# The first loads of a transformer-block kernel: block 3 of x on ScalarE's queue, V's first weights one transfer sooner

## The chip, the cores and the metric

The kernel runs on one core of a Trainium2 chip. Its time is the device time of one execution in microseconds (us), as the median of several runs. A profile of one execution comes with it: its span is counted from the first instruction of the program to the last, and a little time lies around it. Engines are named as in the profile: PE (matmul), PEld (its weight loads), DVE (vector), ACT (scalar, activation functions), POOL (GpSimd) and SP (issues most of the DMAs). "SPq" and "ACTq" are the queues in which SP and ACT issue DMAs.

## The reference

The kernel computes, for one sequence of 2048 rows of 640 values in bfloat16, the row-normalized input xn, and then the sum of x, an attention branch and a gated feed-forward branch, both fed by xn. The attention has 32 heads of 20 values and a sliding window of 256 positions.

```
def _layernorm(x, axis=-1, eps=1e-5):
    m = jnp.mean(x, axis=axis, keepdims=True)
    v = jnp.var(x, axis=axis, keepdims=True)
    return (x - m) / jnp.sqrt(v + eps)
...
        qkv = (x @ wqkv)                   # split in q, k, v of 32 heads
        p = _softmax(where(window of 256, q k^T * 20**-0.5))
        return (p v) @ wo
...
        h = _sigmoid(x @ w_gate) * (x @ w_up)      # 640 -> 1536
        return h @ w_down
...
    xn = _layernorm(A_x)
    return A_x + _A_ref(xn, A_wqkv, A_wo) + _B_ref(xn, ...)
```

## The kernel before

The 2048 rows are worked through in four chunks of 512 rows, and a chunk is four blocks of 128 rows. The order of instructions on every engine is that of the program text (a manual schedule); the framework adds the waits. Only the start of the program matters here, the first chunk until its V projection is done; after that a list of steps interleaves the attention of one chunk with projections and feed-forward work of others, so that PE has always something to do.

**Loads.** The first chunk of x is loaded block by block: `load_rows(s, queue)` (line 156) moves block s, 128 rows of 640 values (160 KB), on the queue that it is given. `load_v(hf)` (line 160) moves one half of V's weights, 400 KB, on SP. `load_wqkv(0)` and `(1)` (line 151) move q's and k's weights, 800 KB each, and then the gate and up weights follow (line 180) and two stores of zeros into scratch (line 177, `clear`). All of these are issued by SP, in this order: block 0, block 1, block 3, V's first half, block 2, V's second half, q, k, gate, up.

**POOL** fills zeros (line 173: 128 partitions of 1536 values, the source of `clear`), makes the identity matrix that the transposes need, fills `neghalf` and `eps` (lines 217 and 219), and then the constant parts of four V tiles (lines 347 and 348).

**ACT** loads the table of the square root and runs a dummy square root on `eps` (line 221), so that the table is there before it is needed.

**PE** first runs eleven dummy matmuls on a constant (line 226, `keep_busy`).

**Normalization of the first chunk** (lines 673 to 710). Blocks 0 and 3 take their statistics on DVE (line 252, two halves of 320 values each, and line 258), the root on ACT (`root`, line 649), the reciprocal and the normalization on DVE (lines 653 and 271). Blocks 1 and 2 take the mean and the sum of squares on ACT (`mean_act`, line 659; `root_act`, lines 664 and 665) and reciprocal and normalization on DVE (lines 669 and 670). Each block is then transposed by five PE instructions (line 277) and copied out of PSUM (line 278: block 0 by ACT in two pieces, the others by DVE). V of a block needs its transposed rows and V's weights: `project_v` (line 353), five matmuls for each half of the weights; the result is copied by ACT or DVE (line 364).

The order of the text interleaves these, and each engine's own order follows from it. DVE: statistics of block 0, normalization of block 0, first half of block 3's statistics, normalization of block 1, second half of block 3's statistics, copy of block 1's transposes, normalization of block 3, and so on. ACT: mean of block 1, root of block 0, squares and root of block 1, copies of block 0's transposes, root of block 3, mean, squares and root of block 2, then copies. PE: dummy matmuls, transposes of block 0, two dummy matmuls, transposes of block 1, V of block 0 (first half of the weights, called v00 below), V of block 1 (first half), transposes of block 3, V of block 0 (second half, v01), V of block 1 (second half), then block 3 with the transposes of block 2 in between, then block 2, and then the q and k projections (line 324).

Each DMA tells of its landing through a semaphore that counts to 16, one for each of 16 DMA engines.

Of the kernel before, what the change touches and what calls it, by code (L numbers as in the profile page):

```python
# [9 lines left out]
P = 128  # L10
# [17 lines left out]
EPS = 1e-5  # L28
# [10 lines left out]
FP32 = mybir.dt.float32  # L39
# [54 lines left out]
def kernel(  # L94
# [11 lines left out]
    nc = tc.nc  # L106
# [4 lines left out]
    def pool(name, bufs, **kw):  # L111
        return ctx.enter_context(tc.tile_pool(name=name, bufs=bufs, **kw))

    const = pool("const", 1)
# [40 lines left out]
    def load_rows(s, queue):  # L155
        queue.dma_start(out=xc[0][:, s, :], in_=xr[:, s, :])  # L156

    def load_v(hf):
        a = hf * HALF
        nc.sync.dma_start(out=wqkv[2][:, :, a:a + HALF], in_=wqkv_r[:, :, 2 * D + a:2 * D + a + HALF])  # L160

    load_rows(0, nc.sync)
    load_rows(1, nc.sync)
    load_rows(3, nc.sync)
    load_v(0)
    load_rows(2, nc.sync)
    load_v(1)
# [1 line left out]
    load_wqkv(1)  # L169

    scratch = {w: tc.dram_tile([H * 32, CW], BF16, name="s" + w) for w in "qk"}
    zero = kp.tile([P, GH, CW], BF16, name="kT")
    nc.gpsimd.memset(zero[:, 0:3, :], 0.0)

# [40 lines left out]
    make_identity(nc, ident)  # L215
    neghalf = const.tile([P, SBC], FP32, name="neghalf")
    nc.gpsimd.memset(neghalf, -0.5)
    eps = const.tile([P, 1], FP32, name="eps")
    nc.gpsimd.memset(eps, EPS)
    scr = const.tile([P, 1], FP32, name="scr")  # L220
    nc.scalar.activation(out=scr, in_=eps, func=SQRT)

    def keep_busy(widths):
        ps = ps_d.tile([P, CW], FP32, name="pwarm", tag="d")
        for n in widths:
            nc.tensor.matmul(ps[:, 0:n], lhsT=ones[:, 0:P], rhs=ones[:, 0:n], start=True, stop=True)
# [623 lines left out]
```

## Time and profile before

| what | value |
| --- | --- |
| median of 3 runs | 308.06 us (308.03 to 308.24) |
| the profiled execution's own time | 308.12 us |
| its span | 306.4 us |
| PE busy | 299.8 us, 98% of the span |
| ACT, DVE, POOL busy | 199.2, 177.6, 177.0 us |
| DMA | 36.87 MB, 120 GB/s on average |
| granted TensorE clock | full throughout |

How to read it: busy times are sums over the whole span. The timeline gives start and duration of an instruction in us from the span's start, its engine, line, operation, the tile that it writes, an arrow and the tiles that it reads, and in brackets the engine's idle time ahead of it with what ended it. The chain of waits is followed back from the last instruction to end: each line has a start, a duration and what the time was spent on. A stretch of the table of windows gives the busy time of each engine in it, the granted clock, the mean busy share of the 16 DMA engines, and the GB/s that they moved.

### The profile page before, as it was taken

Reading aid. Unit: us, or ns where it says so; the run is one execution under the profiler, and the core shown is the slowest. Engines: PE = TensorE matmul, PEld = TensorE weight load, DVE = VectorE, ACT = ScalarE, POOL = GpSimd, SP = SyncE. Lnnn points to the kernel's source line nnn. Section 1 sums busy time; section 2 is a strip of 40 time slices with the busy share of each in tenths; the row PEclk is TensorE's granted clock in tenths of the full one; section 3 lists DMA queues with packets and bytes.
Section 4 is the critical chain, followed back from the end, with each engine's and each line's share of the span. In section 5 each row is a group of like instructions: output and inputs, shape, how many; then the busy total and the mean of one; then the engine's idle time right before and its main releaser. Section 6 shows DMA issues by size and latency. Waiting matters only on the chain.

```text
span 306.4 us, 10016 instructions
## 1 busy us (share of the span) xinstructions
PE 299.8 (98%) x4290; PEld 165.4 (54%) x4325; DVE 177.6 (58%) x355; ACT 199.2 (65%) x198; POOL 177.0 (58%) x317
## 2 busy tenths in 40 slices
PE   7999999999999999999999999999999999999996
PEld 3654444445657654554557654554546665444775
DVE  5735539879675564496946464483733626372434
ACT  6933877698854649888674647878585547778000
POOL 3174687687982927676682728557382847657000
PEclk9999999999999999999999999999999999999999
DMA  7997977886427052810046212740000210000202
GB/s 204 364 328 259 300 201 220 313 242 203 156 90 171 21 181 68 263 50 2 2 132 131 66 58 71 249 142 0 2 2 2 68 43 25 2 2 2 88 21 68
DMA packets 40174, 36.87 MB, mean 120 GB/s; under 512 B 8864, under 2 KB 39840, under 8 KB 40096
## 3 DMA queue, kind: packets, MB, share of 16 engines
q1 hardware_dynamic: 39264, 35.46, 37.6%
q10 hardware_dynamic: 864, 0.75, 0.8%
q8 instruction: 34, 0.56, 0.7%
q14 instruction: 12, 0.10, 0.1%
HBM read 25.59 MB, written 11.44 MB: 121 GB/s over the span
## 4 chain that ended last, share of the span: by engine, by line
PE 96%; DMA 2%; issue 1%; SPq 0%; ACT 0%; ACTq 0%; DVE 0%
PE y L472 18%; PE pu L456 17%; PE pg L449 17%; PE pqk L324 14%; PE ps L529 9%; PE pv L353 7%; PE y L480 7%; PE acc L562 6%; DMA wv<-in_A_wqkv_dram 2%; SPq L156 0%; ACT th L821 0%; PE pt L277 0%; ACTq L496 0%; DVE xn L484 0%
## 5 line engine op out<-in xcount | busy, mean ns | idle before, releaser
L546 POOL TENSOR_SCALAR_AFFINE_SELECT pT<-pT 64x512 bf16<-64x512 bf16 (+1 forms) x256 | 157.0, 613 | 83.4 <-ACT pT L535 71.0
L535 ACT ACTIVATE pT<-ps 128x2048 bf16<-128x2048 f32 (+1 forms) x76 | 141.0, 1855 | 59.4 <-PE ps L529 58.7
L460 DVE SCALAR_TENSOR_TENSOR h<-th,pu 128x512 bf16<-128x512 f32 x48 | 32.7, 680 | 49.8 <-PE pu L456 44.2
L456 PE MATMUL pu<-xnT,wu 128*128 128x512 bf16 x228 | 59.0, 380 | 0.7 <-issue 0.2
L449 PE MATMUL pg<-xnT,wg 128*128 128x512 bf16 x226 | 58.5, 380 | 1.0 <-issue 0.3
L472 PE MATMUL y<-wd,h 128*128 128x320 bf16 (+3 forms) x407 | 56.6, 292 | 0.0
L472 PEld LDWEIGHTS <-h 128*128 128x128 bf16 x407 | 37.1, 98 | 15.3 <-issue 1.8
L452 ACT ACTIVATE th<-pg 128x512 f32<-128x512 f32 x48 | 28.6, 595 | 15.5 <-PE pg L449 15.4
L449 PEld LDWEIGHTS <-wg 128*128 128x128 bf16 x240 | 22.2, 98 | 25.8 <-issue 1.8
L456 PEld LDWEIGHTS <-wu 128*128 128x128 bf16 x240 | 22.0, 98 | 25.5 <-issue 2.0
L529 PE MATMUL ps<-qT,kT 20*64 20x320 bf16 (+4 forms) x1440 | 32.1, 260 | 0.0
L574 DVE STREAM_TRANSPOSE t<-acc 128x512 f32<-128x512 f32 x32 | 21.1, 697 | 17.3 <-PE acc L562 17.3
L529 PEld LDWEIGHTS <-kT 20*64 20x64 bf16 x1440 | 15.4, 103 | 25.0 <-issue 22.4
L484 DVE SCALAR_TENSOR_TENSOR rows<-y,rows 128x320 bf16<-128x320 f32 x30 | 14.5, 487 | 22.9 <-PE y L480 22.7
L586 DVE TENSOR_TENSOR on<-t,rec 128x320 bf16<-128x320 f32 (+4 forms) x48 | 26.0, 542 | 1.1
L353 PE MATMUL pv<-wv,xnT 128*128 128x320 bf16 x160 | 25.6, 300 | 0.1
L480 PE MATMUL y<-wo,oc 128*128 128x320 bf16 (+2 forms) x165 | 24.2, 295 | 0.0
L324 PE MATMUL pqk<-xnT,wk 128*128 128x512 bf16 x97 | 23.0, 380 | 0.2
L324 PE MATMUL pqk<-xnT,wq 128*128 128x512 bf16 x94 | 22.7, 380 | 0.4 <-issue 0.2
L364 DVE CAST v<-pv 64x320 bf16<-64x320 f32 x29 | 14.1, 485 | 11.7 <-PE pv L353 11.4
L562 PE MATMUL acc<-pT,v 64*32 64x320 bf16 (+4 forms) x1440 | 19.7, 253 | 0.0
L562 PEld LDWEIGHTS <-v 64*32 64x32 bf16 x1440 | 16.2, 91 | 5.8 <-issue 1.6
(54 smaller groups left out, 195.4 us busy)
## 6 DMA issues: line engine op xcount, KB each, us to landing
qT<-sq SPq DMA_DIRECT2D x16, 256.0 KB
kT<-sk SPq DMA_DIRECT2D x16, 256.0 KB
sq<-st SPq DMA_DIRECT2D x20, 128.0 KB
sk<-st SPq DMA_DIRECT2D x20, 128.0 KB
out_dram<-rows SPq DMA_DIRECT2D x15, 160.0 KB
wg<-in_B_w_gate_dram SPq DMA_DIRECT2D x4, 480.0 KB
wu<-in_B_w_up_dram SPq DMA_DIRECT2D x4, 480.0 KB
xc<-in_A_x_dram SPq DMA_DIRECT2D x3, 640.0 KB
```

What stands on the lines that cost most here:

```text
L324: nc.tensor.matmul(ps, lhsT=wt[:, m, :], rhs=xnT[c][:, d, :], start=(d == 0), stop=(d == DC - 1))
L353: nc.tensor.matmul(ps[:, 0:HALF], lhsT=xnT[c][:, d, s * P:(s + 1) * P], rhs=wqkv[2][:, d, hf * HALF:(hf + 1) * HALF], start=(d == 0), stop ...
L449: nc.tensor.matmul(pg, lhsT=part(wg, d, f), rhs=xnT[c][:, d, :], start=(d == 0), stop=(d == DC - 1))
L452: nc.scalar.activation(out=th, in_=pg, func=TANH, scale=0.5)
L456: nc.tensor.matmul(pu, lhsT=part(wu, d, f), rhs=xnT[c][:, d, :], start=(d == 0), stop=(d == DC - 1))
L460: nc.vector.scalar_tensor_tensor(out=h, in0=th, scalar=1.0, in1=pu, op0=ADD, op1=MULT)
L472: nc.tensor.matmul(y[:, lo:lo + width], lhsT=ht[c, f][:, s * P:(s + 1) * P], rhs=wd[:, f, cut[0] + lo:cut[0] + lo + width], start=(f == 0) ...
L480: nc.tensor.matmul(y[:, 0:cut[1] - cut[0]], lhsT=oc[c, m][:, s * P:(s + 1) * P], rhs=wo[:, m, cut[0]:cut[1]], start=False, stop=(m == DC - 1))
L529: nc.tensor.matmul(ps[a * U:(a + 1) * U, i, col * U:(col + n) * U], lhsT=qk["k", kc, o // GH][32 * i:32 * i + DH, o % GH + a, kb * U:(kb + ...
L535: nc.scalar.activation(out=pt[:, :, 0:width], in_=ps[:, :, 0:width], func=EXP, scale=SCALE)
L546: nc.gpsimd.affine_select(out=view, in_=view, pattern=[[0, HG], [0, n], [sign, U]], compare_op=GE, fill=0.0, base=base, channel_multiplier ...
L562: nc.tensor.matmul(acc[32 * i:32 * i + 32, q * U:(q + n) * U], lhsT=vt[kb][a * U:(a + 1) * U, u, h * VW:h * VW + 32], rhs=pt[a * U:(a + 1) ...
```

## The change

Three edits, all in the first loads.

- Block 3 of the first chunk is no longer the third load on SP. It is issued by ACT's queue, in the text right behind the dummy square root. On SP, V's first half is now the third load, and everything behind it moves up by one.
- `eps` is filled by POOL ahead of the zeros instead of behind `neghalf`.
- The same instructions run on PE and DVE in the same order. ACT has one more instruction, the DMA issue, between the dummy square root and the mean of block 1; it carries no wait. Lines below the edit shift by up to one in the changed file.

```
     load_rows(0, nc.sync)
     load_rows(1, nc.sync)
-    load_rows(3, nc.sync)
     load_v(0)
     load_rows(2, nc.sync)
     load_v(1)
...
     scratch = {w: tc.dram_tile([H * 32, CW], BF16, name="s" + w) for w in "qk"}
+    eps = const.tile([P, 1], FP32, name="eps")
+    nc.gpsimd.memset(eps, EPS)
     zero = kp.tile([P, GH, CW], BF16, name="kT")
     nc.gpsimd.memset(zero[:, 0:3, :], 0.0)
...
     nc.gpsimd.memset(neghalf, -0.5)
-    eps = const.tile([P, 1], FP32, name="eps")
-    nc.gpsimd.memset(eps, EPS)
     scr = const.tile([P, 1], FP32, name="scr")
     nc.scalar.activation(out=scr, in_=eps, func=SQRT)
+    load_rows(3, nc.scalar)
```

More of the change, by code (lines that the diff above doesn't have):

```diff
@@ L163 @@
     load_rows(1, nc.sync)
-    load_rows(3, nc.sync)
     load_v(0)
@@ L171 @@
     scratch = {w: tc.dram_tile([H * 32, CW], BF16, name="s" + w) for w in "qk"}
+    eps = const.tile([P, 1], FP32, name="eps")
+    nc.gpsimd.memset(eps, EPS)
     zero = kp.tile([P, GH, CW], BF16, name="kT")
@@ L217 @@
     nc.gpsimd.memset(neghalf, -0.5)
-    eps = const.tile([P, 1], FP32, name="eps")
-    nc.gpsimd.memset(eps, EPS)
     scr = const.tile([P, 1], FP32, name="scr")
     nc.scalar.activation(out=scr, in_=eps, func=SQRT)
+    load_rows(3, nc.scalar)
     def keep_busy(widths):
```

## Prediction

> **What bounds the kernel now.** I read the page first: PE is busy for 299.8 of 306.4 us, and the chain that ended last is PE for 96% and DMA for 2%. So time can be won or lost only where PE stands still. I listed its gaps: all are ahead of 7.1 us, except some of 0.05 or 0.16 us, where a matmul record is missing ("x4" for five), and the drain of the last stores. The rest is a full queue: a shift of PE at 11 us arrives whole at the end, unless a new wait swallows it. So I worked out only the first 11 us.
>
> The chain in order of time, for the first 12 us:
>
> ```profile
> 1.71 0.43 SPq L156
> 2.14 0.04 issue
> 2.18 4.88 DMA wv<-in_A_wqkv_dram
> 7.06 0.04 issue
> 7.10 1.52 PE pv L353 x10
> 8.62 0.28 PE pt L277 x5
> 8.90 1.77 PE pv L353 x13
> 10.66 0.28 PE pt L277 x5
> ```
>
> The first V matmul (v00) starts when the first half of V's weights lands, 7.06. That load is SP's fourth issue, behind three 160 KB blocks of x; the block-3 issue ahead of it is the 1.71 line. Removing it brings V's issue from 2.18 to 1.71: 0.47 us. But see how little is behind the wait, in the timeline:
>
> ```profile
> 5.25 0.49 DVE L252 BATCH_NORM_STATS2 stats<-xc 128x6 f32<-128x320 bf16 x1
> ...
> 5.50 0.29 ACT L665 ACTIVATE rstd<-rstd,eps 128x1 f32<-128x1 f32 x1
> ...
> 5.83 0.16 DVE L669 RECIPROCAL rstd<-rstd 128x1 f32<-128x1 f32 x1
> ...
> 6.03 0.45 DVE L670 TENSOR_SCALAR xn<-xc,neg,rstd 128x640 bf16<-128x640 bf16 x1
> ...
> 6.53 0.45 PE L277 MATMUL pt<-ident,xn 128*128 128x128 bf16 x5 [0.41 <-DVE xn L670]
> ...
> 7.10 1.52 PE L353 MATMUL pv<-wv,xnT 128*128 128x320 bf16 x10
> ```
>
> The five transposes of block 1, ahead of v00 in PE's queue, start at 6.53. Such a run occupies PE 0.28 us before a V matmul follows (the chain's 8.62 0.28). So v00 could start at 6.81: the weights hold it for **0.29 us, and no more can be won there**, though the load comes 0.47 sooner. Behind the weights stands block 1: landed by 3.64 (ACT's wait ends there), then ACT's mean, square and root, DVE's normalization, the transposes, each instruction released by the one before. A block 1 late by d makes v00 possible at 6.81+d.
>
> **Next waits on PE's way.** The ten V matmuls and block 3's transposes keep their own pace: transposes 1.36 us after v00, the next V matmuls (v01, second half of the weights) 0.28 later. By the trace's semaphore counts that second half landed complete at 8.61, and v01 started at 8.74, so without a sooner landing only 0.09 can be passed on there (8.61+0.04=8.65). Block 2's transposes stand 1.76 after v01, at 10.50; their input was written at 9.85+0.45=10.30, and 0.06 later (as from 6.03+0.45 to 6.53, rounded up) is 10.36. That chain goes back through ACT (root 7.15, mean of block 2 at 7.51) to DVE's statistics of block 3. It moves with d, except for 0.07: ACT was free at 7.44 and block 2 landed at 7.49. So block 2's transposes cannot start before 10.29+d: 0.21 us before today with d=0. **The end moves by the larger of PE's own shift and d-0.21.**
>
> **Part by part.**
> 1. Epsilon ahead of the zeros. POOL does the same instructions; the 0.10 us memset goes from 2.67 to about 0.80. The zeros, 1.38 us, identity and V memsets come up to 0.10 later at first. The identity is ready at 2.69 and used at 5.39; the zeros' DMA is issued at 8.73. No cost, cover over 2 us. The gain is on ACT: its dummy SQRT waits for epsilon 0.72 us, to 2.80; ACT's next input comes at 3.64, so of itself this saves nothing. It frees the DMA issue written behind the SQRT.
> 2. One ACT issue more: 0.36 to 0.45 us (the four at 282.98 to 284.81). Block 1 is not there before 3.64, so an issue ending by then costs ACT nothing; held to 2.8 it would still end at 3.25.
> 3. SP: one issue fewer. V's first weights 0.47 sooner, block 2, V's second half, wq, wk likewise up to the 1.66 us issue at 4.27, where the queue is full (the DMAs are busy 0.98 and more from 5 us on). Each still has its landing bound by the bytes ahead.
> 4. When does block 3 start? Unshown: no ACT issue stands behind a table load in this trace. The nearest row is this:
>
> ```profile
> 281.75 1.88 ACT L535 ACTIVATE pT<-ps 128x2048 bf16<-128x2048 f32 x1 [0.87 <-PE ps L529]
> 282.98 0.87 ACTq L491 DMA_DIRECT2D rows<-in_A_x_dram  x2
> 283.52 0.59 ACT L452 ACTIVATE th<-pg 128x512 f32<-128x512 f32 x1
> ```
>
> The tanh at 283.52 is ahead of the DMAs in ACT's program. Its wait for PE ended at 282.87; then ACT's queue issued the DMA at 282.98, while the exp still ran and the tanh had not begun. So a wait holds the queue, a busy engine does not. Early bound: epsilon done at 0.90, block 3 issued at about 1.0, beside the table load (0.80 to 2.09). Late bound: the load holds it, 2.1 to 2.3. I take the **early one**, nearest to that row. Then block 3 is no longer behind block 1 (SP issue 1.25) but ahead of it.
>
> 5. What that does to block 1. Busy share of the DMAs and GB/s are the last two columns here:
>
> ```profile
> 1.75:2.00 0.25, 0.25 (x2) 0.05 (x1) 0.00 (x0) 0.25 (x1) 0.25 (x1) 1.00 0.41 61
> 2.00:2.25 0.25, 0.25 (x2) 0.15 (x1) 0.00 (x0) 0.09 (x1) 0.25 (x2) 1.00 0.66 143
> 2.25:2.50 0.25, 0.25 (x2) 0.00 (x0) 0.00 (x0) 0.00 (x0) 0.17 (x2) 1.00 1.03 369
> ...
> 2.75:3.00 0.25, 0.25 (x2) 0.07 (x1) 0.00 (x0) 0.20 (x1) 0.25 (x7) 1.00 1.00 369
> ...
> 3.75:4.00 0.25, 0.25 (x2) 0.15 (x1) 0.23 (x1) 0.25 (x1) 0.00 (x0) 1.00 0.47 54
> 4.00:4.25 0.25, 0.25 (x2) 0.04 (x1) 0.21 (x1) 0.25 (x1) 0.00 (x0) 1.00 0.55 105
> ```
>
> From 2.25 to 3.5 the engines are nearly full. Before 2.25 some 51 thousand bytes moved ((61+143)x0.25); the other 440 of the three blocks' 491 take 1.19 us at 369 GB/s: the last byte at 3.44. In this trace the last packet of the three ended at 3.77 and block 3 landed at 4.08, 0.31 behind; block 1, issued last of the three, would land at 3.44+0.31=3.75 against 3.62: **d=0.13**, between 0 (block 3 takes only idle time) and 0.46 (block 1 lands where block 3 did, 4.08; issue to landing was 2.37 us for both). Block 0 may be late by 0.15 at no cost: its statistics end at 4.23, and its root waits for ACT until 4.38.
> Beside it, a sentence that carries nothing: the Trainium skill, "DMA: Bandwidth & Descriptors", section "Issuing engines are not separate DMA queues", says that transfers from either issuer interleave on the same 16 engines and only issue time is saved; it speaks against the gain, and by it alone the weights would land with the same bytes ahead of them and the sum would come to no change.
>
> **Sum** with d=0.13: V's first weights, 0.47 sooner less some sharing, land between 6.59 and 7.06; if by 6.90, v00 starts at 6.81+0.13=6.94. Block 3's transposes follow at 8.30, v01 at 8.58 (8.65 if the second half still lands at 8.61), so PE could reach block 2's transposes at 10.34 to 10.41; their input lets them start at 10.29+0.13=10.42 against 10.50: **-0.08 us**. The profiled execution is 308.12 (span 306.41 and 1.71 around it), 0.06 over the median of 308.06; so 308.04 for it, 308.0 for the median.
>
> **Rivals.**
> - A, the forecast: most of the gain is lost to the later block 1; over d=0.1 to 0.46 the end moves by -0.1 to +0.25: 307.95 to 308.3, from d=0.21 on no gain. Chance 0.55.
> - B, the gain comes: block 3 uses idle engines (the 0.47 and 0.55 shares at 3.75 to 4.25 speak for it) or is issued at 2.1 and lands 2.37 later, 4.5, before its use at 5.25. Then d=0, v00 at 6.81, and the end moves by -0.09 (second half still at 8.61) to -0.21: 307.85 to 307.97. Against it: full engines. Chance 0.25.
> - C, slower: block 3 is issued at 2.1 or later, and the engines serve V's first weights ahead of it. DVE needs block 3 at 5.25 and has 0.09 to spare (5.74 to 5.83) before block 1's reciprocal, which is queued behind; then block 1's transposes and v00 wait. Block 3 landing at r gives d=r-5.34; it decides from r=5.55, costs 0.2% from 6.17, and at worst (V's 6.59 plus 0.44 for its own eight packets per engine, 55 ns each in the trace) r=7.03, +1.48: 309.5. For it: block 2, behind V's weights on SP, took 4.83 us. Against it: a separate queue, and the early issue. Chance 0.13, half of it beyond 0.2%.
> The Trainium skill, same page, section "Queues, rings and completion order", has an engine drain a run of some 9 to 17 descriptors of one ring before it switches; that rule leans to C. No run here shows two rings sharing yet.
> - D, it does nothing: V's weights land at 7.06 as now, since the bytes ahead are the same, and d is under 0.2; 308.06. Chance 0.07.
>
> About 0.2% (0.6 us) is what a measurement of this kernel can tell from no change. A, B and D lie inside; beyond it are half of C and some unforeseen delay of the first loads. PE's gaps before 7.1 us make a gain of 0.6 all but impossible. Slower 0.10, faster 0.02, same 0.88. Range: A and B, and C up to its half, 307.8 to 308.6.
>
> **What would show it.** In the changed profile: ACT's DMA issue beside the table load (1.0) or behind it (2.1); the start of ACT's mean of block 1 (3.64 now: d directly); V's issue at 1.71; the first V matmul (6.94 in A, 6.81 in B, over 7.1 in C); block 2's transposes against 10.50, and the same difference at the end. DVE's statistics of block 3 later than 5.25 with block 1 on time would mean C. A different shift at the end than at 10.50 would refute that the rest is a full queue.

## The result, and the profile after

| | before | after |
| --- | --- | --- |
| median of the runs | 307.96 us (307.89 to 308.24) | 309.05 us (308.92 to 310.14) |
| the profiled execution's own time | 308.12 us | 308.92 us |
| its span | 306.4 us | 307.2 us |
| granted TensorE clock | full throughout | full throughout |

The changed kernel is slower: the ratio of the times is 1.0038, with an interval from 1.0026 to 1.005. The medians differ by 1.09 us, the two profiled executions by 0.80. That of before lay 0.16 above its median and that of after 0.13 below, so the two traces account for 0.80, and the other 0.29 is spread over executions that left no trace.

The chain of waits of after, for its first 12 us (start, duration, what the time was spent on), no longer begins with V's weights:

```profile
1.25 3.12 DMA xc<-in_A_x_dram
4.37 0.02 issue
4.39 0.83 ACT xn L659 x2
5.22 0.19 ACT rstd L649
5.41 0.82 ACT xn L664 x2
...
6.78 0.46 DVE xn L670
7.24 0.05 issue
7.29 0.45 PE pt L277 x5
7.74 1.44 PE pv L353 x10
9.18 0.28 PE pt L277 x5
9.46 1.77 PE pv L353 x13
11.22 0.28 PE pt L277 x5
```

Before, the end hung on a load that SP issued at 2.18 and that landed at 7.06. Now it hangs on block 1, issued at 1.25 and landed at 4.37, and on everything that is done to it: mean, root, squares, normalization, transposes. V's weights do not appear any more. The timeline shows the same from the side of the instructions:

```profile
0.80 1.28 ACT L220 ACT_TABLE_LOAD   x1 [0.80 <-PEq L834]
0.94 0.38 ACTq L156 DMA_DIRECT2D xc<-in_A_x_dram  x1
...
3.54 0.89 DVE L252 BATCH_NORM_STATS2 stats<-xc 128x6 f32<-128x320 bf16 x2 [3.54 <-DMA xc<-in_A_x_dram]
4.39 0.74 ACT L659 ACTIVATE xn<-xc 128x640 bf16<-128x640 bf16 x1 [2.10 <-DMA xc<-in_A_x_dram]
```

ACT's queue issued block 3 at 0.94, while the table load ran (0.80 to 2.08). The mean of block 1 began at 4.39 and not at 3.64: block 1 was late by 0.75. Block 0's statistics began at 3.54, where they began at 3.10 before: block 0 was late too. From the semaphore counts of the two traces, the times at which the last of 16 counts came:

| landed complete | before | after |
| --- | --- | --- |
| block 0 | 3.08 | 3.52 |
| block 3 | 4.08 | 3.93 |
| block 1 | 3.62 | 4.37 |
| V's weights, first half | 7.06 | 6.27 |
| block 2 | 7.49 | 6.72 |
| V's weights, second half | 8.61 | 7.85 |

So the change did what its text says: V's first half came 0.79 sooner. But block 3 was served whole between block 0 and block 1. From block 0 to block 1 it took 0.54 before and 0.85 after, 0.31 more; the other 0.44 of the 0.75 is that block 0 itself came later. The table of windows shows that part. Its last two columns are the busy share of the DMAs and the GB/s, as in the prediction's table of before:

```profile
1.75:2.00 0.25, 0.25 (x2) 0.05 (x1) 0.00 (x0) 0.25 (x1) 0.25 (x1) 1.00 1.02 92
2.00:2.25 0.25, 0.25 (x2) 0.15 (x1) 0.00 (x0) 0.24 (x2) 0.25 (x2) 1.00 0.66 97
2.25:2.50 0.25, 0.25 (x3) 0.00 (x0) 0.00 (x0) 0.05 (x1) 0.17 (x2) 1.00 0.54 97
2.50:2.75 0.25, 0.25 (x2) 0.15 (x1) 0.00 (x0) 0.00 (x0) 0.25 (x3) 1.00 0.63 179
2.75:3.00 0.25, 0.25 (x2) 0.07 (x1) 0.00 (x0) 0.00 (x0) 0.25 (x7) 1.00 1.03 379
```

Where before reached 369 GB/s at 2.25, after moved 97, and 179 in the quarter behind it, although there was more to move. The packets show how: of those that began before 2.6 us, 12 took over 300 ns, up to 764, where before had one, of 331; the usual packet of a block takes 55. Three other kernels with one queue (the runs with one more instruction on ACT, with `eps` alone and with the order 0, 3, 1) had 4 to 7 such packets, none over 382: the change brings longer ones more than it brings more of them.

With that, block 2's transposes began at 11.06 instead of 10.50. From there on PE's shift stayed at 0.55 up to 46 us. Then a **second part** came: from 48.96 to the end the shift is 0.80. It begins at the exp on ACT that frees PSUM for PE's scores. ACT in before:

```profile
44.68 0.60 ACT L452 ACTIVATE th<-pg 128x512 f32<-128x512 f32 x1 [0.25 <-PE pg L449]
46.15 1.88 ACT L535 ACTIVATE pT<-ps 128x2048 bf16<-128x2048 f32 x1 [0.87 <-PE ps L529]
```

and in after:

```profile
45.23 0.60 ACT L452 ACTIVATE th<-pg 128x512 f32<-128x512 f32 x1 [0.25 <-PE pg L449]
47.03 1.88 ACT L535 ACTIVATE pT<-ps 128x2048 bf16<-128x2048 f32 x1 [1.20 <-POOL pT L546]
```

The tanh is later by 0.55, the exp by 0.88. In brackets the exp's idle time grew from 0.87 to 1.20, and the releaser's name changed to POOL. That name is a coincidence: the POOL instruction that ended at 46.93 in after is the one that ended at 46.37 in before, where the exp had begun at 46.15 without it. PE's count, the true releaser, came at 46.62 in after. ACT then stood for about 0.4 us with its input ready. Counted from 0 in the order of the trace, waits included, this exp is ACT's instruction 62 in before and 63 in after. In both traces ACT pauses at its instruction 63. In before that is a wait behind the exp, recorded 0.33 us after the exp's start; in after the same wait is number 64 and comes 0.03 after it. So in before the pause hides behind the exp's 1.88 us. The DMA issue that the change gives ACT moved the pause onto the exp, for which PE waits.

### The profile page after: what moved, and what is told of

It reads as the page before. It is cut to its first block, busy times and chain, and to the rows that moved or that the text cites. A ratio compares the mean times of both kernels' runs of the same rounds, so it can differ in the third digit from the quotient of the medians.

```text
span 307.2 us, 10051 instructions
## 1 busy us (share of the span) xinstructions
PE 302.4 (98%) x4325; PEld 165.5 (54%) x4325; DVE 177.6 (58%) x355; ACT 199.1 (65%) x198; POOL 177.3 (58%) x317
## 4 chain that ended last, share of the span: by engine, by line
PE 94%; ACT 2%; DMA 1%; POOL 1%; DVE 0%; issue 0%; SPq 0%
PE y L472 17%; PE pu L456 17%; PE pg L449 17%; PE pqk L324 15%; PE ps L529 9%; PE pv L353 7%; PE y L480 7%; PE acc L562 6%; ACT pT L535 1%; DMA xc<-in_A_x_dram 1%; POOL pT L546 1%; DMA out_dram<-xn 0%; PE pt L277 0%; ACT xn L659 0%; ACT xn L664 0%
## 5 line engine op out<-in xcount | busy, mean ns | idle before, releaser
L456 PE MATMUL pu<-xnT,wu 128*128 128x512 bf16 x240 | 59.8, 380 | 0.0
L449 PE MATMUL pg<-xnT,wg 128*128 128x512 bf16 x240 | 59.8, 380 | 0.0
```

Of the source, the lines that this page charges most:

```text
L449: nc.tensor.matmul(pg, lhsT=part(wg, d, f), rhs=xnT[c][:, d, :], start=(d == 0), stop=(d == DC - 1))
L456: nc.tensor.matmul(pu, lhsT=part(wu, d, f), rhs=xnT[c][:, d, :], start=(d == 0), stop=(d == DC - 1))
```

## The experiments

The **theory** had three statements. (1) Block 3, issued early, is served whole ahead of block 1, which is what PE then waits for. (2) Block 0 is late because two loads start at once from two queues. (3) The added instruction moves ACT's pause onto the exp at 47 us. The rivals: the loss at the start is due to the order of the transfers alone, whatever the queue; or the delay of block 0 comes from a second queue as such; and the second part comes from POOL, as the profile's bracket says, or just follows from the shift of 0.55. Times are medians, the ratios are against runs of the kernel before on the same chip (308.08, then 308.0, then 307.99 us in the three groups below). Shifts are against the profiled execution of before.

### Epsilon late

`eps` goes back behind `neghalf`; the rest of the change stays, so ACT's issue waits.

```
-    eps = const.tile([P, 1], FP32, name="eps")
-    nc.gpsimd.memset(eps, EPS)
     zero = kp.tile([P, GH, CW], BF16, name="kT")
...
     nc.gpsimd.memset(neghalf, -0.5)
+    eps = const.tile([P, 1], FP32, name="eps")
+    nc.gpsimd.memset(eps, EPS)
```

> The changed kernel with epsilon filled in its old place, behind the identity: ACT's queue can issue block 3 only at about 2.8 us (epsilon was done at 2.77 before), behind SP's blocks 0 and 1 and its V weights. Theory (the changed kernel lost 0.56 us because block 3 was issued at 0.94, ahead of block 1, and 0.25 us because one more instruction in ACT's stream puts an instruction-fetch pause ahead of an exp at 47 us): block 1 lands as before (ACT's mean of it starts at 3.64), block 3 lands 2.4 us after its issue plus up to 0.44 of sharing, 5.2 to 5.6, the shift at block 2's transposes is -0.2 to +0.1 us, and the 0.25 stays: -0.05 to +0.35 us in all. Rival (the engines serve V's weights ahead of another queue's block): block 3 lands at 6.3 or later, DVE's statistics of it start a microsecond late, and the kernel is 1 us or more slower than before.

Measured: 313.4 us, ratio 1.0162 (1.014 to 1.0184). The timeline:

```profile
3.11 0.44 ACTq L156 DMA_DIRECT2D xc<-in_A_x_dram  x1
...
9.25 0.49 DVE L252 BATCH_NORM_STATS2 stats<-xc 128x6 f32<-128x320 bf16 x1 [3.91 <-DMA xc<-in_A_x_dram]
...
10.35 0.71 PE L277 MATMUL pt<-ident,xn 128*128 128x128 bf16 x5 [4.22 <-DVE xn L670]
```

Block 1 was on time (its mean at 3.65). Block 3, issued at 3.11, landed at 9.23, behind both halves of V's weights (6.76 and 8.30), the second of which SP had issued at 2.75. DVE waited 3.91 us for it with block 1's normalization queued behind, and PE stood still for 4.22. The theory's landing at 5.2 to 5.6 was wrong and its rival right. That is the mechanism of rival C of the prediction, beyond its worst case, a landing at 7.03. A second cost came on top: the granted clock fell to 0.50 from 8.26 on, for 6.83 us, so that the matmuls from 9 to 15 us ran at half pace. In the row of 9 to 11 us the granted clock is the third number from the end:

```profile
9.00:11.00 2.00, 0.65 (x6) 0.66 (x7) 1.61 (x5) 0.03 (x1) 0.00 (x0) 0.50 1.06 379
```

It follows that the early `eps` is what makes the moved load bearable at all: without it the change costs some 5 us, the halved clock included.

### Epsilon in the middle

After, with `eps` filled between the zeros and the identity, so that ACT issues block 3 at about 2.2.

```
-    eps = const.tile([P, 1], FP32, name="eps")
-    nc.gpsimd.memset(eps, EPS)
     zero = kp.tile([P, GH, CW], BF16, name="kT")
     nc.gpsimd.memset(zero[:, 0:3, :], 0.0)
+    eps = const.tile([P, 1], FP32, name="eps")
+    nc.gpsimd.memset(eps, EPS)
...
     make_identity(nc, ident)
```

> The changed kernel with epsilon filled behind the zeros and ahead of the identity: ACT's queue issues block 3 at about 2.3 us, behind block 1 (1.25) and V's first weights (1.70) of SP. Theory (block 1 was late because block 3 was issued ahead of it): ACT's mean of block 1 starts at 3.6 to 3.7, block 3 lands at 4.7 to 5.2, in time for its use at 5.25, V's weights land before 6.8; the shift at block 2's transposes is -0.1 to -0.2 us, plus 0.25 for ACT's added instruction: +0.05 to +0.15 us in all. Rival (a second queue in the first microseconds delays the first loads whatever the order): block 1 is late by 0.3 us or more again, and the kernel is slower than before by 0.4 us or more.

Measured: 309.4 us, ratio 1.0041 (1.0026 to 1.0055).

```profile
1.70 0.43 SPq L160 DMA_DIRECT2D wv<-in_A_wqkv_dram  x1
...
2.25 0.38 ACTq L156 DMA_DIRECT2D xc<-in_A_x_dram  x1
...
3.62 0.74 ACT L659 ACTIVATE xn<-xc 128x640 bf16<-128x640 bf16 x1 [1.17 <-DMA xc<-in_A_x_dram]
...
6.87 0.49 DVE L252 BATCH_NORM_STATS2 stats<-xc 128x6 f32<-128x320 bf16 x1 [1.55 <-DMA xc<-in_A_x_dram]
...
7.96 0.45 PE L277 MATMUL pt<-ident,xn 128*128 128x128 bf16 x5 [1.35 <-DVE xn L670]
```

Block 1 is on time (3.62), so with block 3 out of the way d is nothing, which speaks for (1). But block 3, issued 0.55 behind V's first half, landed at 6.84, behind it (6.70). The landing between 4.7 and 5.2 that the theory had expected was wrong, and so was the rival's late block 1. Block 2's transposes shifted by 1.23, and the exp at 48 added another 0.22, as in after. The Trainium skill, "DMA: Bandwidth & Descriptors", section "Queues, rings and completion order", has an engine change rings after a run of typically 9 to 17 descriptors. The prediction counted that rule for C, though it would let block 3's eight packets per engine in after one run of V's 40, and block 3 landed 0.14 behind all of them. Nor were the two loads served one after the other: 23 of block 3's 128 packets began before V was finished on any engine (4.64). The first of them began at 3.90, yet no engine was done with its eight before 4.96, where eight in a row take 0.44. So statement (1), a load served whole, holds here for blocks of eight packets per engine, not for a block beside V's 40.

### One more instruction on ACT

The kernel before, with its dummy square root written twice: nothing else moves.

```
     nc.scalar.activation(out=scr, in_=eps, func=SQRT)
+    nc.scalar.activation(out=scr, in_=eps, func=SQRT)
```

> The kernel before with its dummy square root written twice: one more instruction in ACT's stream, done by 3.3 us while ACT waits for block 1 until 3.64, and nothing else. Theory (an added ACT instruction puts a pause of instruction fetch ahead of the exp at 46 us): no shift at 10.5 us, the exp at 46.1 starts 0.3 us later, and everything behind is 0.2 to 0.3 us later, so the kernel is 0.25 us slower. Rival (the second part of the shift came from the first part, by another meeting of the engines): the same time as before within 0.1 us.

Measured: 308.38 us, ratio 1.001 (1.0001 to 1.0018). ACT at 46 us (lines are one further down in this kernel):

```profile
46.16 1.88 ACT L536 ACTIVATE pT<-ps 128x2048 bf16<-128x2048 f32 x1 [1.18 <-POOL pT L547]
```

In this execution V's first half happened to land at 6.39, and PE ran 0.295 ahead of before up to 46 us. Yet the exp began at the old time, with the same false releaser in its bracket; behind it PE was only 0.069 ahead. So one instruction more costs 0.226 us at this place, without any change of the loads. That the lead is not lost there anyway is seen in the run with `eps` alone: its lead of 0.23 passes 46 us whole. Statement (3) holds.

### The order 0, 3, 1 on SP alone

The kernel before, with only the order of the loads changed: no second queue, no added instruction.

```
     load_rows(0, nc.sync)
+    load_rows(3, nc.sync)
     load_rows(1, nc.sync)
-    load_rows(3, nc.sync)
```

> The kernel before with blocks 0, 3, 1 issued by SP in this order: block 3 ahead of block 1 on one queue, V's weights as before, no instruction added to ACT. Theory (the order counts): block 1 lands where block 3 did, at about 4.08, ACT's mean of it starts 0.46 us later, block 2's transposes 0.25 us later, and the kernel is 0.25 us slower, with no second part at 47 us. Rival (the second queue counts, not the order): a loss much smaller than 0.25 us; if block 1 is late by 0.75 us as in the changed kernel, +0.54 us, then the queue has no part in it.

Measured: 310.05 us, ratio 1.0055 (1.0034 to 1.0076), where +0.25 us had been expected. Block 1, now the third load, landed at 4.93, its mean began at 4.96, and PE stood still for 2.07 us ahead of block 0's transposes at 6.70. Then the clock fell. In the rows of the windows it is the third number from the end, again:

```profile
4.96 0.74 ACT L659 ACTIVATE xn<-xc 128x640 bf16<-128x640 bf16 x1 [1.95 <-DMA xc<-in_A_x_dram]
...
6.00:7.00 1.00, 0.30 (x6) 0.30 (x7) 0.96 (x3) 0.97 (x3) 0.00 (x0) 1.00 1.14 341
7.00:8.00 1.00, 0.85 (x7) 0.27 (x5) 0.87 (x4) 0.83 (x3) 0.00 (x0) 0.51 0.99 314
8.00:9.00 1.00, 1.00 (x8) 0.76 (x7) 0.80 (x3) 0.54 (x2) 0.00 (x0) 0.50 1.08 399
9.00:10.00 1.00, 1.00 (x6) 0.52 (x5) 0.68 (x4) 0.97 (x3) 0.00 (x0) 0.50 1.07 392
```

From 7.02 the clock was halved for 3.41 us, and block 2's transposes began at 12.78. The shift then stayed as it was: there is no second part at 47, as (3) demands of a kernel without the added instruction. What the order alone costs at the end this run does not tell, since the halved clock covers it. But it does tell d: without a second queue block 1 was late by 1.32, more than the 0.75 of the change. Before's 4.08 for the third load on SP was an early landing: with the same three loads in the old order, block 3 landed at 4.70, 4.73 and 4.87 in the runs with one more instruction on ACT, with the small load and with `eps` alone. So the rival that the order alone makes block 1 late is not excluded by its size; the split of the 0.75 into 0.31 and 0.44 is that of one execution.

### Two more instructions behind the change

After, with two more dummy exps on ACT near 16 us. They carry ACT's pause past the exp, if (3) is right.

```
+    nc.scalar.activation(out=scr, in_=neghalf[:, 0:1], func=EXP)
+    nc.scalar.activation(out=scr, in_=neghalf[:, 0:1], func=EXP)
```

> The changed kernel with the dummy exp that follows the V copies written three times: two more instructions in ACT's stream, at 16 us, where ACT waits until 19.8. Theory (ACT's stream pauses for about 0.35 us at its 64th instruction; in the kernel before an exp stands just ahead of that place, in the changed kernel it stands behind it, and with two more a tanh that waits for PE anyway is there): the shift at block 2's transposes is as in the changed kernel, +0.56 us, and the second part at 47 us, +0.25, is gone: +0.56 us in all against before. Rival (the second part comes from the later start itself): +0.8 us as in the changed kernel.

Measured: 309.71 us, ratio 1.0052 (1.0038 to 1.0066). At 46 us it is as (3) says: the releaser is PE again, the idle time 0.87 again, and the shift is that of the start, 0.53.

```profile
46.68 1.88 ACT L535 ACTIVATE pT<-ps 128x2048 bf16<-128x2048 f32 x1 [0.87 <-PE ps L529]
```

But the time did not fall, for a new loss of 0.46 appeared at 130 us. The chain there:

```profile
130.03 0.33 PE ps L529 x17
130.36 0.25 issue
130.60 0.23 PE ps L529 x7
```

PE stood still for 0.25 us in the middle of a run of scores, waiting for nothing that the profile shows. In the trace, a 16 KB load of instructions, taken to be PE's, that began at 127.25 took 2.07 us; in before and after the same one took 1.05 and 0.98. At the end, the last store was issued 0.99 later than in before, like all around it, but took 2.09 us to land instead of 1.46: 0.63 more. So the second part's place was found, and with it out of the way two other losses stood in its stead.

### Block 1 instead of block 3 on ACT

After, with blocks 1 and 3 exchanged: SP loads 0, 3, then V; ACT issues block 1 at 0.94.

```
-    load_rows(1, nc.sync)
+    load_rows(3, nc.sync)
...
-    load_rows(3, nc.scalar)
+    load_rows(1, nc.scalar)
```

> The changed kernel with blocks 1 and 3 exchanged between the queues: SP issues 0, 3, V's first half, 2; ACT's queue issues block 1 at 0.94. Theory (loads are served whole, in the order of their arrival, whichever queue they are on, and the first load of a second queue beside the first one makes all of the first packets slow): block 1 takes the place that block 3 had in the changed kernel, landing at 3.9, so ACT's mean of it starts 0.3 us later than before, block 2's transposes +0.1 us, with the 0.25 of ACT's added instruction +0.3 to +0.4 us in all. Rival (the second queue costs nothing, only the order did): block 1 lands at 3.4 to 3.6, the shift at block 2's transposes is -0.1 to -0.2, in all +0.05 to +0.15.

Measured: 308.58 us, ratio 1.0016 (1.0007 to 1.0025).

```profile
3.79 0.74 ACT L659 ACTIVATE xn<-xc 128x640 bf16<-128x640 bf16 x1 [1.50 <-DMA xc<-in_A_x_dram]
```

Block 0 landed at 3.34, block 1 at 3.77, and its mean began at 3.79, so d is 0.15. Block 2's transposes began at 10.47, 0.03 ahead of before. The second part was there (0.24 at 48 us), so the shift at the end was +0.21. The order of arrival decides the first part: with block 1 second in line, it is gone. The profiled execution (308.32) lies 0.26 under the median, and what the other executions lost beyond it no trace shows.

### Epsilon behind a third of the zeros

After, with the zeros filled in two pieces and `eps` between them: ACT issues block 3 at 1.40, between SP's block 1 (1.25) and V (1.70).

```
+    nc.gpsimd.memset(zero[:, 0:1, :], 0.0)
     eps = const.tile([P, 1], FP32, name="eps")
     nc.gpsimd.memset(eps, EPS)
-    nc.gpsimd.memset(zero[:, 0:3, :], 0.0)
+    nc.gpsimd.memset(zero[:, 1:3, :], 0.0)
```

> The changed kernel with epsilon filled between the first third of the zeros and the rest (one POOL instruction more), so that ACT's queue issues block 3 at about 1.4 us: behind block 1 (1.25) and ahead of V's first weights (1.70). Theory (served whole in order of arrival): blocks land in the order 0, 1, 3, V as before; block 1 at 3.6, block 3 at 4.0 to 4.9, in time, V's weights at 6.3 to 6.9; the shift at block 2's transposes is -0.1 to -0.2 us, plus 0.25 for ACT's added instruction: +0.05 to +0.15 us in all. Rival (any second queue in the first microseconds slows the first packets): blocks 0 and 1 are 0.3 us late or more, and the sum is +0.35 us or more.

Measured: 308.89 us, ratio 1.0036 (1.0016 to 1.0056). Landings: block 0 at 3.20, block 1 at 3.96, block 3 at 4.51, V's first half at 6.62. The order of arrival is that of the issues, as (1) says. Yet block 1 was still 0.35 late, 0.12 of it with block 0; where the rest comes from this trace does not settle. Block 2's transposes shifted by 0.15; with 0.22 at 48 us the profile's end shifted by 0.37. The median is 0.5 above that, beyond what the profile shows.

### A small load on ACT's queue

The kernel before with `eps` early, and ACT loads 128 x 8 values of x that nobody reads.

```
     nc.scalar.activation(out=scr, in_=eps, func=SQRT)
+    spare = const.tile([P, 8], BF16, name="spare")
+    nc.scalar.dma_start(out=spare, in_=xr[:, 15, 0:8])
```

> The kernel before with epsilon ahead of the zeros and, on ACT's queue behind the dummy square root, a load of 128 x 8 values (16 bytes a partition) that nobody reads; SP's order as before. It adds almost no bytes. Theory (the second queue's opening at 0.94 beside the first one slows the first packets): block 0 lands at 3.3 to 3.5 instead of 3.08 and block 1 at about 3.9, the shift at block 2's transposes is about +0.1 us, with ACT's added instruction +0.35 us. Rival (only the 160 KB ahead of block 1 did it): block 0 at 3.1 and block 1 at 3.65, +0.25 us in all, from ACT's instruction alone.

Measured: 308.65 us, ratio 1.0022 (1.0014 to 1.0031). Block 0 landed at 3.16 and block 1 at 3.58, 0.08 later and 0.04 sooner than in before. A second queue that starts at the same time is therefore not what delays the blocks; that part of the theory, (2) in its bare form, falls. The loss in this profile is +0.18 at block 2's transposes, since V's first half landed at 7.23 here, and 0.22 at 48 us, where ACT again has one instruction more; another 0.15 comes later, up to the end.

### The change with one copy fewer

After, with ACT's two copies of block 0's transposes made one: ACT has as many instructions as before.

```
-    for lo, hi in ((0, 3), (3, DC)):
+    for lo, hi in ((0, DC),):
```

> The changed kernel with ACT's two copies of block 0's transposes made one, so that ACT has as many instructions as before in spite of the added DMA issue. Block 0's transposed rows are ready later by 0.1 us at most, while the first V matmul waits for block 1 until 7.6. Theory (ACT's stream pauses about 0.35 us at its 64th instruction, and one instruction more put an exp behind that place): the shift at block 2's transposes stays +0.56 us, the second part at 47 us is gone: +0.56 us in all. Rival (the second part belongs to the later start or to the second queue): +0.8 us as in the changed kernel.

Measured: 308.99 us, ratio 1.0031 (1.0018 to 1.0043).

```profile
46.95 1.88 ACT L535 ACTIVATE pT<-ps 128x2048 bf16<-128x2048 f32 x1 [0.87 <-PE ps L529]
```

The pause at the exp is gone: its shift, 0.80, is that of the start, 0.81. (Block 1's mean began at 4.65 in this execution, 0.26 later than in that of after.) But 0.26 came at 130 us, as with the two added exps: PE stood still, and the instruction load there took 2.14 us. So the median hardly differs from that of after, and it is the trace, not the time, that speaks for (3) here.

### Block 1 on ACT, with one copy fewer

Both of the edits that had removed something, together: the block 1 order above and the single copy.

```
-    load_rows(1, nc.sync)
+    load_rows(3, nc.sync)
...
-    load_rows(3, nc.scalar)
+    load_rows(1, nc.scalar)
...
-    for lo, hi in ((0, 3), (3, DC)):
+    for lo, hi in ((0, DC),):
```

> ACT's queue issues block 1 instead of block 3 at 0.94 (SP: 0, 3, V's first half, 2), and ACT's two copies of block 0's transposes are one, so that ACT has as many instructions as before. With two copies the shift at block 2's transposes was -0.03 us and the pause at 46 us cost 0.24. Theory (order of arrival and ACT's count are all there is): no second part, -0.1 to +0.2 us in all, since block 1 then lands at 3.6 to 3.9 as a load in the same place. It is the version most likely to beat the kernel before, by 0.1 us at best. Rival (a second queue costs by itself): +0.3 us or more with no second part.

Measured: 308.16 us, ratio 1.0002 (0.9994 to 1.0011). Block 1's mean began at 3.73, block 2's transposes at 10.42, 0.08 ahead of before. No second part followed, and the profiled execution, 308.04, was 0.08 under that of before. Against the same order with two copies the median's loss fell from 0.58 to 0.17 us, so here (3) is seen in the times too. This is the best form of the change that the runs found, and it cannot be told from the kernel before.

### Epsilon alone

The kernel before with nothing but `eps` ahead of the zeros.

```
+    eps = const.tile([P, 1], FP32, name="eps")
+    nc.gpsimd.memset(eps, EPS)
     zero = kp.tile([P, GH, CW], BF16, name="kT")
...
     nc.gpsimd.memset(neghalf, -0.5)
-    eps = const.tile([P, 1], FP32, name="eps")
-    nc.gpsimd.memset(eps, EPS)
```

> The kernel before with epsilon ahead of the zeros and nothing else: the loads and ACT's instructions as before. Theory: the dummy square root ends at 2.3 instead of 3.0, nobody waits for it, 0.0 us, within 0.15 of the kernel before. Rival (POOL's order matters): a shift in the first 12 us.

Measured: 308.07 us, ratio 1.0 (0.9991 to 1.0009). The edit of `eps` costs nothing and brings nothing by itself. In this execution V's first half landed at 6.39 with the old order on SP, and block 2's transposes began at 10.27, 0.23 ahead of before; from 86 us on only 0.10 of the lead was left. So this lead did not arrive whole.

### A whole block on ACT's queue that nobody reads

The kernel before with `eps` early, and ACT loads 160 KB of x's last block into a tile that is overwritten later.

```
     nc.scalar.activation(out=scr, in_=eps, func=SQRT)
+    nc.scalar.dma_start(out=wd[:, 0, :], in_=xr[:, 15, :])
```

> The kernel before with epsilon ahead of the zeros and a 160 KB load of x's last block on ACT's queue at 0.94, into memory that is overwritten later; SP's order as before. Theory (any whole block that arrives between blocks 0 and 1 is served whole before block 1, and two such loads at once make the first packets slow): block 0 lands at 3.4 to 3.5, block 1 at 4.3 to 4.4, ACT's mean of block 1 starts 0.7 us later, +0.8 us or more in all, since V's weights are as late as before and behind one block more. Rival (only the order counts): block 0 at 3.1, block 1 at 4.05, the mean 0.4 us later. Rival (a load that nobody waits for takes idle engines only): block 1 at 3.6 to 3.7.

Measured in one execution: 309.07 us. Here three blocks stay on SP as before.

```profile
0.94 0.38 ACTq L222 DMA_DIRECT2D wd<-in_A_x_dram  x1
...
3.40 0.89 DVE L253 BATCH_NORM_STATS2 stats<-xc 128x6 f32<-128x320 bf16 x2 [3.40 <-DMA xc<-in_A_x_dram]
```

Block 0 landed at 3.38, the unread block at 3.78, block 1 at 4.29. The shift was 0.55 at block 2's transposes and 0.22 more at 48 us, nearly the whole loss of after. V's first half landed at 7.37, but did not hold V's first matmul: that began at 7.56, 0.29 behind block 1's transposes (7.27), as in after. Block 3, now the fourth load, landed at 6.15 and held DVE for 0.17 us, so a small share of the 0.55 is its own. With the small load, the delay of block 0 is 0.08, with a whole block 0.30: (2) holds in the form that a second *large* load must start beside the first. Which load it is matters too, for a reason that no run shows: block 0 landed at 3.44 to 3.77 in the three kernels with block 3 on ACT at 0.94, at 3.29 to 3.38 in the three with another whole block there, and at 3.00 to 3.20 in the other eight.

## Why the prediction was wrong, step by step

**The step that failed first is part 5**, the size of d. It put d at 0.13 with an upper bound of 0.46; block 1 was late by 0.75. The bound came from the engines' rate: the bytes of three blocks at 369 GB/s, and block 1 no later than block 3 had been. Both took block 0 as given and the start of the transfers as in before, and the bound rested on one landing of the third load, 4.08, where other executions had 4.70 to 4.93. The runs show two terms in its place. Block 3 is served whole, ahead of block 1: 0.31 more between the landings of block 0 and block 1. And block 0 came 0.44 later, since with two large loads at once the engines moved 97 GB/s at 2.25 where 369 had been counted on. The unread block reproduces most of both (block 0 late by 0.30, block 1 by 0.67).

**The second is part 2**, which valued ACT's added issue at nothing because it ends before block 1 lands. It does, by 0.94+0.38=1.32. What it costs is its place in the count: 0.25 us at 48 us, since ACT's pause fell on the exp that PE waits for. The added square root showed 0.226 for this without any other change, and the merged copy took it away. With that the sentence "The end moves by the larger of PE's own shift and d-0.21" failed as well: 0.56 at block 2's transposes and 0.80 at the end. The prediction had named a different shift at those two places as what would refute its full queue. It did refute it, at one place; from 8 to 46 us and from 49 us on the shift was constant. For a lead the full queue failed at another place: with `eps` alone 0.13 of 0.23 us was lost before 86 us.

The rest stands:

- The 0.29 us that could be won, and block 1 as next in line: v00 was forecast at 6.81+d, 7.56 with the measured d, and began at 7.58. But the 0.29 was that of one execution: with the old order on SP, v00 began at 6.72 and 6.79 in the runs with one more instruction on ACT and with `eps` alone, where V's first half had landed at 6.39. There nothing was left to win.
- The price d-0.21: 0.54 against 0.56 measured in after, 0.14 against 0.15 with `eps` behind a third of the zeros, -0.06 against -0.03 with block 1 on ACT.
- Part 1, `eps` at no cost: shown by the run with that edit alone.
- Part 3, V's issue 0.47 sooner: 1.70. The landing, 6.27, was sooner than the 6.59 given as its earliest, and was of no use. How much of this is the change is open: with the unchanged order on SP, V's first half landed between 6.39 and 7.23 in executions of other kernels.
- Part 4, the early issue beside the table load: 0.94.

Of the rivals, A named the mechanism of the loss but ended at +0.25, the value of its largest d. B failed with d. C is not what happened in after, where block 3 landed at 3.93. But it is real: with `eps` in the middle its formula gives 6.84-5.34-0.21=1.29, and 1.23 was measured. D failed, since the weights did come sooner. Neither failed step alone would have passed the 0.6 us that the prediction took for the limit of the measurement: the first is worth 0.55 and the second 0.25. Together they are 0.80 in the traces, and 1.09 in the medians.

The Trainium skill, "DMA: Bandwidth & Descriptors", section "Issuing engines are not separate DMA queues", says that only issue time is saved by a second issuer. The traces agree that nothing more was gained (block 1 on ACT with one copy fewer: ratio 1.0002), and show besides that the second issuer's load can take the place of another (block 3 landed at 3.93, ahead of block 1 at 4.37).

Two things stay open: why the first packets take up to 764 ns when two 160 KB loads begin together (in before, on one queue, V's load has packets of up to 1216 ns, at 4.45), and why the instruction load at 126 to 127 us takes between 0.93 and 2.14 us. Both are seen in the traces; no run took their cause apart. Nor does any trace show why ACT pauses, or what the 0.29 us is that the medians differ by beyond the traces.

## What to carry to other kernels

A load that is moved to an idle engine's queue is not free: in these traces a block was served in the order of arrival, so ask first which load it now overtakes, and move the one whose user waits longest (here block 1, not block 3). When the chain's first wait is worth 0.29 us and the next one in line is a load too, forecast the new landing of that load with its start taken as uncertain, not only with a full rate behind an old start. And an added instruction has a second price in where it pushes an engine's later stalls: compare the shift of the critical engine at several places along the trace, and do not trust a releaser's name where the idle time jumps by some 0.3 us.

## What the hardware showed that was not expected

- **The clock falls after idle time at the start.** With the order 0, 3, 1, PE stood still from 4.63 to 6.70, and from 7.02 on the granted clock was 0.50 for 3.41 us. With `eps` late it stood still from 6.13 to 10.35, and the clock was 0.50 from 8.26 on, for 6.83 us. With a gap of 1.35 us (`eps` in the middle) and of 0.81 us (after) it stayed full. That the idling is the cause fits these four, and was not tried by itself.
- **ACT pauses at its instruction 63**, by 0.33 us in before, and this shows only where an instruction on PE's path stands there: 0.22 to 0.25 us in each of the kernels with one instruction more. At 319 the traces show a pause of some 0.3 us too, which holds up no store; at 127, 191 and 255 none is to be seen.
- **A long instruction load can stop PE.** The one at 126 to 127 us (in before's time) took 0.93 to 1.87 us in eleven traces, and PE lost nothing there; it took 2.02, 2.07 and 2.14 in the other three (`eps` late, two more instructions, one copy fewer), and in these PE fell back by 0.22 to 0.46 us at 130 us.
- **The same order of loads lands differently in different executions**: V's first half between 6.39 and 7.23 us, and the block ahead of it between 4.08 and 4.87, with no edit ahead of them on SP.
